# Moving two slabs of sure tokens ahead of the last row sums, with more filler behind them and a fixed hand-over to the experts

## The chip, the cores and the metric

The kernel runs on one core of a Trainium2 chip. The metric is the device time of one execution in microseconds (us); several executions are timed in rounds next to executions of the kernel before on the same chip. A ratio is the mean time of one kernel's fast runs over that of the other's fast runs of the same rounds, so it is not quite the ratio of the medians that are quoted. All runs told here were classed fast, that is, within 1.5% of the fastest of the same kernel. The kernel before shows two clusters among its fast runs, about 262.8 and about 263.9 us.

The engines: PE is TensorE's matmul, DVE VectorE, ACT ScalarE, POOL GpSimd (which issues most of the transfers here), SP the sync engine. PSUM is the memory, in banks, into which matmuls write and from which ACT and DVE copy. Moments are us from the start of the profiled execution.

## The reference

Attention with a linear bias and a sparse mask (8 global keys and a local window of 96) gives 3072 tokens of 512 numbers; a balanced router then hands each token to one of eight experts, 384 tokens each, in the order of all logits; each expert is a two-layer network.

```python
scores = q @ k.T / sqrt(D) - slopes * dist          # only global or local keys kept
x = softmax(scores) @ v                             # 3072 tokens x 512
order = argsort(-(x @ w_gate).flatten())
for idx in order:                                   # each token once, at most 384 a expert
    tok, e = idx // E, idx % E
    if assigned[tok] < 0 and counts[e] < cap: assigned[tok] = e; counts[e] += 1
for e in range(8):
    out[assigned == e] = relu(x[assigned == e] @ w1[e]) @ w2[e]
```

## The kernel before

The tokens of the first batches are known before the last batch's attention is done. So for five experts a first slab of 128 "sure" tokens is picked early (names with E at the end): small matmuls find their ids, an indirect DMA gathers each slab, PE transposes it, and its two layers (up, down) are used as filler for PE while the router's rounds wait for DVE. Cuts are marked "# ...".

```python
def e8_pe(q4):                       # one of three groups of six small matmuls: the ids
    # ...
def e8_ids():                        # two DVE ops, then one gather for each of four slabs
    # ...
    for e in range(ER): early_rows(e)

# the end of attention, in fixed order
            pr = sums(13)
            sums_out(13, pr)
            mask(15, 2)
            for g in range(3):
                attend(14, g)
                e8_pe(g)
            # ...
            e8_ids()
            pr = sums(14)
            # ...
            av(15)
            # ...
            pr = sums(15)            # 48 sum matmuls, then 8 for the gates
            sums_out(15, pr)

# filler: a list of (price in us, action); work(us) takes items until the price is spent
def rows(e):    # 4 transposes of slab e, ACT copies them to SBUF, price 0.25; two PSUM buffers
def up_one(...) # one matmul of the first layer, price 0.078; ACT applies relu after 16
def down_one(...)  # one matmul of the second layer, price 0.22; ACT evicts after 8
def work(us):
    while us > 0.0:
        cost, go = items.pop(0); go(); us -= cost

# the router: work(0.7), four rounds, the dispatch
def fast_round(k, X, Dg):            # PE -> DVE -> PE -> DVE ..., filler in between
    # ... work(0.34), work(1.0 or 1.1), comparisons tg on DVE, then
            work(0.7)
dispatch()                           # ids of all tokens, work(3.2) inside
for e in range(ER): gather(e, range(1, TSLAB), False)
# ...
while items: work(0.1)               # what is left of the filler

# the experts, outside the fixed order: the scheduler places the transposes
load_x(0)                            # slabs 1 and 2 of expert 0: transpose, DVE copy
```

The third expert's weights, two loads of 1 MB, are issued by POOL about 118.9 and 119.7 us, before the gathers of the sure slabs.

The softmax here doesn't subtract the row's maximum and nothing guards it: scores larger than these inputs give would overflow.

## Time and profile before

| | |
|---|---|
| median | 262.9 us (262.85 to 263.75) |
| span of the profiled run, clock | 261.1 us, 0.99 |
| PE busy | 242.8 us, 93% |
| last row sums end, router's first matmul (pkn) | 142.77, 144.54 |
| rounds one; two to four | 5.27; 15.88 us |
| last sure down matmul has been issued; experts start | 180.49; 182.62 |

### The profile page before, as it was taken

To read this page: it belongs to the slowest core of one execution; us is meant where nothing else is said; L and a number is where in the kernel's file an instruction comes from. 1 tells how busy PE (TensorE), PEld (TensorE's weight loads), DVE (VectorE), ACT (ScalarE), POOL (GpSimd) and SP (SyncE) were. 2 spreads that over 40 slices of the span, in tenths; PEclk is the share of its full clock that TensorE was granted. 3 is DMA by queue.
4 is the path that set the end of the run, shared out by engine and by line. 5 is a ranking of instruction groups with operands and counts; after the bars stand their busy time and mean duration, and the time that the engine had idled before them with its cause. 6 is when DMAs were issued, how large, how long until landed. Compare 5 with 4: busy or idle time off the path is not lost.

```text
span 261.1 us, 7832 instructions
## 1 busy us (share of the span) xinstructions
PE 242.8 (93%) x3319; PEld 179.9 (69%) x3331; DVE 163.0 (62%) x347; ACT 144.1 (55%) x245; POOL 87.9 (34%) x147
## 2 busy tenths in 40 slices
PE   8799979999999999999999899998999999999960
PEld 2567867888788888887787677664777765555520
DVE  3987998897978989689873877771223223223120
ACT  5998959679596895963442422233444432441600
POOL 5050000030270592014008400147865684541240
PEclk9999999999999999999999999999999999999996
DMA  6993597659698498949996999923799999991221
GB/s 261 335 318 76 165 251 209 189 103 270 177 248 239 93 292 188 208 93 148 210 211 143 155 188 215 241 95 102 132 242 268 276 240 229 201 281 41 89 84 46
DMA packets 52570, 49.29 MB, mean 189 GB/s; under 512 B 29745, under 2 KB 44081, under 8 KB 52529
## 3 DMA queue, kind: packets, MB, share of 16 engines
q0 software_dynamic: 15680, 26.22, 48.9%
q1 hardware_dynamic: 36848, 22.50, 31.2%
q8 instruction: 28, 0.46, 0.7%
q14 instruction: 14, 0.11, 0.1%
HBM read 56.05 MB, written 9.44 MB: 251 GB/s over the span
## 4 chain that ended last, share of the span: by engine, by line
PE 48%; DVE 20%; issue 10%; ACT 8%; DMA 6%; POOL 4%; POOLq 0%; SPq 0%; DVEq 0%
PE po L443 9%; PE ps L390 7%; PE ph L1375 5%; DVE RT L330 5%; DVE P L423 5%; PE po L1384 5%; PE pr L474 5%; DMA out_dram<-ot,idi 4%; POOL out_dram L945 4%; PE pk L519 3%; PE poE L988 3%; DMA RT<-in_q_dram 2%; ACT qT L355 2%; PE phE L972 2%; ACT P L408 2%
## 5 line engine op out<-in xcount | busy, mean ns | idle before, releaser
L408 ACT ACTIVATE P<-ps 128x860 f32<-128x860 f32 (+1 forms) x46 | 39.2, 891 | 23.1 <-PE ps L390 22.4
L1378 ACT ACTIVATE hT<-ph 128x256 bf16<-128x256 f32 (+1 forms) x64 | 27.1, 423 | 39.3 <-PE ph L1375 37.3
L390 PE MATMUL ps<-qT,kA 32*128 32x215 f32 (+2 forms) x864 | 43.3, 333 | 1.6 <-ACT qT L355 1.6
L443 PE MATMUL po<-P,v 128*64 128x215 f32 (+6 forms) x576 | 41.5, 293 | 0.2 <-DVE P L423 0.2
L390 PEld LDWEIGHTS ps<-qT,kA 32*128 32x128 f32 x864 | 36.8, 185 | 6.2 <-issue 2.8
L443 PEld LDWEIGHTS po<-P,v 128*64 128x64 f32 x576 | 34.0, 136 | 8.7 <-issue 3.8
L423 DVE TENSOR_TENSOR P<-P,Wm 128x860 f32<-128x860 f32 (+1 forms) x32 | 32.9, 1043 | 6.6 <-ACT P L408 3.9
L330 DVE STREAM_TRANSPOSE RT<-RT 128x768 f32<-128x768 f32 x28 | 26.2, 959 | 3.5 <-DMA RT<-in_k_dram 3.4
L474 PE MATMUL pr<-P,onesx 128*32 128x168 f32 (+11 forms) x768 | 27.6, 259 | 0.0
L1391 DVE COPY ot<-po 128x512 f32<-128x512 f32 x18 | 12.4, 691 | 24.1 <-PE po L1384 24.1
L945 POOL DMA_INDIRECT out_dram<-ot,idi x19 | 18.7, 983 | 26.0 <-DVE ot L1391 20.0
L1355 DVE COPY xT<-pxe 128x512 bf16<-128x512 bf16 x19 | 7.4, 421 | 31.6 <-PE pxe L1354 31.1
L474 PEld LDWEIGHTS pr<-P,onesx 128*32 128x32 f32 x768 | 24.7, 109 | 2.3 <-issue 0.3
L1384 PEld LDWEIGHTS <-hT 128*128 128x128 bf16 x152 | 14.4, 98 | 15.5
L340 ACT COPY kA<-RT 128x720 f32<-128x720 f32 (+2 forms) x18 | 24.3, 1352 | 0.2
L1375 PE MATMUL ph<-xT,w 128*128 128x384 bf16 (+1 forms) x160 | 23.4, 305 | 0.0
L1384 PE MATMUL po<-w,hT 128*128 128x512 bf16 x99 | 22.8, 379 | 0.2
L937 POOL DMA_INDIRECT xe<-x_tok,idi x19 | 18.3, 962 | 10.8 <-issue 4.3
L448 ACT COPY oT<-po 128x384 f32<-128x384 f32 x32 | 14.7, 486 | 11.4 <-PE po L443 11.4
L1375 PEld LDWEIGHTS <-w 128*128 128x128 bf16 x160 | 15.6, 98 | 7.7
L416 DVE TENSOR_TENSOR P<-P,Wm 128x860 f32<-128x860 f32 x16 | 16.4, 1058 | 6.7 <-ACT P L408 6.7
L519 PE MATMUL pk<-ident,oT 128*128 128x128 f32 x96 | 16.7, 288 | 2.4 <-DVE LT L490 2.2
(241 smaller groups left out, 328.1 us busy)
## 6 DMA issues: line engine op xcount, KB each, us to landing
w<-in_moe_w_dram POOLq DMA_DIRECT2D x10, 1024.0 KB, 12.2
v<-in_v_dram SPq DMA_DIRECT2D x32, 180.0 KB
RT<-in_k_dram SPq DMA_DIRECT2D x7, 768.0 KB
RT<-in_q_dram SPq DMA_DIRECT2D x7, 768.0 KB
w_early<-in_moe_w_dram POOLq DMA_DIRECT2D x8, 512.0 KB, 7.9
x_tok<-x SPq DMA_DIRECT2D x32, 96.0 KB
RT<-in_moe_w_dram POOLq DMA_DIRECT2D x2, 1024.0 KB, 18.3
w_early<-in_k_dram SPq DMA_DIRECT2D x1, 768.0 KB
```

The source lines that it names most:

```text
L330: nc.vector.transpose(out=t, in_=src[:, :, 32 * g : 32 * g + 32])
L340: nc.scalar.copy(out=kA[:, i0:i1, 8:128].rearrange("p i (c j) -> p i c j", j=NJ), in_=t[:, i0 * NC5 : i1 * NC5, :].rearrange("p (i c) j -> ...
L390: nc.tensor.matmul(heads[a][:, o : o + w], lhsT=kA[r, gd, i, :], rhs=qTt[r, gd, KT * i : KT * i + w], start=(gd == 0), stop=(gd == 1), ski ...
L408: nc.scalar.activation(P[:, :, 0 : GW[g]], ps[w_][:, :, 0 : GW[g]], AF.Exp, scale=0.125)
L423: tt(out=P[:, :, 0 : GW[g]], in0=P[:, :, 0 : GW[g]], in1=Wm[:, h0 : h0 + 2, lo : lo + GW[g]], op=ALU.mult)
L443: nc.tensor.matmul(po[n][bk][64 * t : 64 * t + 64, a - QB * bk : z - QB * bk], lhsT=v7[:, t, i, :], rhs=P[:, t, o + a - q0 : o + z - q0], ...
L474: nc.tensor.matmul(o_, lhsT=l_, rhs=r_, start=first[gq], stop=True, skip_group_check=True)
L519: nc.tensor.transpose(pk[:, bb, :], oTs[n][:, 3 * hf + bb].rearrange("c g r -> c (g r)"), ident)
L945: s = nc.gpsimd.indirect_dma_start(out=out[:, :], out_offset=bass.IndirectOffsetOnAxis(ap=ids, axis=0), in_=ot, in_offset=None)
L1375: nc.tensor.matmul(ph[:, 0 : 128 * ns], lhsT=w1_of(e)[:, kc, 128 * fc : 128 * fc + 128], rhs=xT_e[:, kc, 0:ns, :].rearrange("p t n -> p (t ...
L1378: nc.scalar.activation(hT[:, fc, 0 : 128 * ns], ph[:, 0 : 128 * ns], AF.Relu)
L1384: nc.tensor.matmul(po, lhsT=hT[:, fc, 128 * j : 128 * j + 128], rhs=w2_of(e)[:, fc, :], start=(fc == 0), stop=(fc == NFC - 1))
```

## The change

Its intent: have the ids of the sure slabs two us sooner, so that two slabs can be transposed ahead of the last row sums; with those out of the way, have up matmuls ready as filler in front of round one and in its waits; and transpose the first expert's own slabs in fixed order while the last filler runs. The whole diff, but for lines that only move a declaration:

```diff
@@ the end of attention
             pr = sums(13)
+            e8_pe(0)
+            e8_pe(1)
             sums_out(13, pr)
+            attend(14, 0)
+            e8_pe(2)
+            e8_ids()
             mask(15, 2)
-            for g in range(3):
-                attend(14, g)
-                e8_pe(g)
+            attend(14, 1)
+            attend(14, 2)
             oT_out(14, 0)
             oT_out(14, 1)
-            e8_ids()
             pr = sums(14)
             sums_out(14, pr)
             e7_flags()
             av(15)
+            px = ps_s.tile([128, 2, NKC, 128], BF16, tag="ps0", name="px")
+            for e in range(2):
+                for kc in range(NKC):
+                    nc.tensor.transpose(px[:, e, kc, :], xe_early[e][:, 128 * kc : 128 * kc + 128], ident_bf)
             oT_out(15, 0)
             oT_out(15, 1)
+            for e in range(2):
+                nc.scalar.copy(out=xT_early[e], in_=px[:, e])
             pr = sums(15)
@@ the order of the filler
-        for e in range(ER):
-            rows(e)
-        for f, e in ((up, 0), (up, 1), (down, 0), ...
+        for f, e in ((rows, 2), (up, 0), (rows, 3), (up, 1), (down, 0), ...
@@ a round
             for k0 in range(0, k, 4):
+                if k > 4:
+                    work(0.3)
                 nc.vector.tensor_tensor(   # tg
@@
-            work(0.7)
+            work(0.9)
@@ ahead of round one
-            work(0.7)
+            work(1.5)
@@ the tail
+            while len(items) > 4:
+                work(0.1)
+            rows_of_first(1, "pk")
             while items:
                 work(0.1)
+            rows_of_first(2, "pr2")      # 4 transposes into a free bank, DVE copy
@@ the experts
-            load_x(0)
             if not first:
                 gather(0, slabs(0))
+                load_x(0)
```

More of the change, by code (lines that the diff above doesn't have):

```diff
@@ L930 @@
     xes = {}
+    xT_of = {}
     scatters = []
@@ L999, in down @@
                 down_one(e, fc)
-        for e in range(ER):
-            rows(e)
-        for f, e in ((up, 0), (up, 1), (down, 0), (up, 2), (down, 1), (rows, 4), (up, 3), (down, 2), (up, 4), (down, 3),
-                     (down, 4)):
+        for f, e in ((rows, 2), (up, 0), (rows, 3), (up, 1), (down, 0), (up, 2), (down, 1), (rows, 4), (up, 3), (down, 2),
+                     (up, 4), (down, 3), (down, 4)):
             f(e)
@@ L1331, in routing, with rows_of_first @@
             nc.vector.tensor_single_scalar(out=fi, in_=fm, scalar=0.0, op=ALU.is_gt)
+            def rows_of_first(t, tag):
+                if t == 1:
+                    xT_of[0] = fp.tile([128, NKC, TSLAB, 128], BF16, tag="xT_e", name="xT_0")
+                xe = xes.pop(t)
+                pxe = ps_d.tile([128, NKC, 128], BF16, tag=tag, name=f"pxe{t}")
+                for kc in range(NKC):
+                    nc.tensor.transpose(pxe[:, kc, :], xe[:, 128 * kc : 128 * kc + 128], ident_bf)
+                nc.vector.tensor_copy(out=xT_of[0][:, :, t - 1, :], in_=pxe)
+            while len(items) > 4:
+                work(0.1)
+            rows_of_first(1, "pk")
             while items:
                 work(0.1)
+            rows_of_first(2, "pr2")
             while deferred:
@@ L1342, in experts @@
             ps_o = fctx.enter_context(tc.tile_pool(name="ps_o", bufs=3, space=bass.MemoryType.PSUM))
-            xT_of = {}
             def slabs(e):
@@ L1359, in experts @@
                 gather(0, slabs(0))
-            load_x(0)
-            if not first:
+                load_x(0)
                 gather(1, slabs(1))
```

## The prediction

> **What bounds the kernel now.** I read the page first, then the chain of work that ended last in order of time, then the time windows around the router, then the waits of TensorE. The page says TensorE is the engine:
>
> ```profile
> PE 242.8 (93%) x3319; PEld 179.9 (69%) x3331; DVE 163.0 (62%) x347; ACT 144.1 (55%) x245; POOL 87.9 (34%) x147
> ...
> PE   8799979999999999999999899998999999999960
> ```
>
> PE is near full in every slice, so a change pays only where it takes idle time off PE; moving its work about pays nothing by itself. From 182.62 us, where the experts' first matmul starts, to 250 us the windows show PE busy 66.95 of 67.38 us; after that only the last eviction, scatter and landing follow. So the end is the start of the experts plus a constant, and the question is how much earlier that start (182.6) comes. The windows in front of it (columns: window, its length, then busy time and count per engine; the first pair is PE):
>
> ```profile
> 138.32:140.78 2.46, 2.46 (x40) 2.15 (x37) 1.76 (x6) 0.48 (x1) 1.95 (x2) 1.00 0.72 168
> 140.78:142.77 1.99, 1.99 (x60) 1.61 (x57) 0.00 (x0) 0.48 (x1) 1.42 (x2) 1.00 0.27 80
> 142.77:144.54 1.77, 1.00 (x15) 0.73 (x13) 1.39 (x6) 1.28 (x3) 1.77 (x3) 1.00 0.43 134
> 144.54:149.81 5.27, 4.61 (x52) 3.81 (x52) 4.39 (x16) 1.82 (x5) 2.17 (x4) 1.00 1.01 154
> 149.81:155.05 5.24, 5.07 (x55) 4.12 (x56) 4.21 (x17) 1.43 (x5) 0.00 (x0) 1.00 1.16 184
> 155.05:160.35 5.30, 5.22 (x48) 3.88 (x49) 4.31 (x17) 1.56 (x4) 0.00 (x0) 1.00 1.17 213
> 160.35:165.69 5.34, 5.17 (x54) 3.99 (x53) 4.15 (x17) 1.51 (x4) 1.14 (x2) 1.00 1.17 214
> ...
> 180.66:182.62 1.96, 0.93 (x12) 0.75 (x12) 0.76 (x2) 0.58 (x1) 1.50 (x2) 1.00 0.46 134
> ```
>
> Attention (to 142.77) leaves PE no gap. The idle time is 0.77 before the router's first round, 0.66 in that round, 0.17, 0.08 and 0.17 in the other three, about 0.3 spread over 165.7 to 180.7, and 1.03 at the hand-over to the experts: 3.2 us in all. That is the most this change can earn. Who PE waited for, between 126 and 190 us:
>
> ```profile
> PE pxe L1354 <- ACT otE L992: 0.7, 1, 0.7
> PE px L959 <- ACT RT L960: 0.5, 1, 0.5
> PE prk L1117 <- DVE tg L1111: 0.4, 2, 0.2
> PE pxe L1354 <- DVE xT L1355: 0.4, 1, 0.4
> PE pkn L1075 <- DVE Lb L505: 0.3, 1, 0.3
> PE X L1060 <- DVE Dg L1138: 0.2, 1, 0.2
> ```
>
> And the hand-over in the chain (start, length, what): the last sure-token matmul, its eviction, the first transposes that wait for that eviction, their copy, then the experts.
>
> ```profile
> 179.19 1.47 PE poE L988 x6
> 180.69 0.59 ACT otE L992
> 181.33 0.40 PE pxe L1354 x4
> 181.82 0.43 DVE xT L1355
> 182.29 0.38 PE pxe L1354 x4
> 182.68 3.60 PE ph L1375 x32
> ```
>
> **What the Trainium skill says.** "TensorE: Matmul & The Clock Gate", section "Wait — 56ns, not 53.3ns?", gives a warm start-to-start of 55.6 ns for 128 columns and 215.7 for 512. The trace agrees: 32 up matmuls (phE) take 1.79 us in the chain, 56 ns each, and nine down matmuls (poE) take 1.94 us, 216 ns each. The same page, "Part 4: PE-mode transpose": the result lands in PSUM and needs a copy. Here four transposes take 0.22 us of PE and the copy 0.42 us on DVE or 0.58 on ACT; that copy is the price of the hand-over. "Perfetto Trace Analysis", section "Tensor Engine Instruction", says PE's ends are modelled: a matmul of 56 ns is recorded as 219 ns here, so busy time hides part of each gap, and I count from start to start below. "DMA: Bandwidth & Descriptors", section "Queues, rings and completion order": each DMA engine consumes a ring in order. The gathers of the sure tokens stand behind the third expert's weights, issued by the same engine at 119.0 and 119.7; the second of these took 20.6 us to land (about 140.3), and DMA share is above 1.1 until 139 us. So ids two us sooner need not mean rows two us sooner.
>
> **The change part by part.**
>
> 1. Ids. Now idiE is done at 136.81 and the first gather issues at 137.10. Moved up, the three id groups (0.38 us of PE each in the chain) run at sums(13)'s end, 132.45: two groups 0.76, attend(14,0) 0.88, last group 0.38, so about 134.5; two DVE ops (0.17 each) give ids at about 134.95, 1.9 sooner. DVE's mask(15,2) moves from 133.91 to about 135.0 and is wanted near 139.9. PE does the same work in another order. Gain by itself: 0.
>
> 2. Two slabs transposed before sums(15). Eight transposes, 0.44 us, now lie ahead of the last row sums, so the router's DVE chain (LT to Lb, then pkn at 144.54) moves to about 144.98. They leave the queue of filler behind it. This is a cost of 0.44 on the chain, bought back by part 3.
>
> 3. The gap before round one. From sums(15)'s end to pkn there are 1.66 us. Before, three slabs (0.66 us of PE, with a 0.5 us stall for the third slab's PSUM buffer) fill it. After: one slab (0.22), then 1.25 of nominal budget at 0.078 is 17 up matmuls, 0.95 us. Work done there 1.17, of which the chain paid 0.44 as shift: net 1.17 + 0.44 - 0.66 - 0.44 = 0.51 us gained.
>
> 4. Round one. It takes eight candidates, so DVE's two tg comparisons (1.29 us) and the selection bound it. Filler before: one slab plus 10 ups, then 9 ups: 1.28 us. After: 13 ups 0.73; 0.3 is two ups and a slab 0.33; 0.3 is four ups 0.22; 0.9 is twelve ups 0.67: 1.95. The extra 0.67 lies almost wholly in the 0.66 that PE waits. The fourth slab now sits between two uses of the same two PSUM buffers, so the second expert's first up waits some 0.25 us for the ACT relu; it falls inside DVE's comparison. Gain about 0.6.
>
> 5. Rounds two to four. Each has 0.2 more budget, and the order is further on (more downs at 216 ns). Estimated filler 1.93, 1.96, 1.99 us against 1.62, 1.98, 1.78 now; idle there is 0.42 in sum. Gain about 0.25; the rest lengthens rounds by 0.1 to 0.2, which costs nothing as it shortens the tail. Ids of the main dispatch come about 0.9 later than now (173.68 to about 174.6).
>
> 6. Hand-over. The last down matmul has been issued by 180.49; the experts start at 182.62: 2.13 us, in it 12 transposes (0.66), so 1.47 lost. After: slab one is transposed four downs before the end, slab two right behind the last down into a bank freed long before. From slab two's start, copy begins 0.49 later (as 181.33 to 181.82 now), takes 0.42, and a matmul starts 0.04 on: 0.97, in it 0.22 of work. Lost: 0.75, or 0.53 if the next expert's slab slips into the gap. Gain 0.7 to 0.95, say 0.8.
>
> Sum: 0.51 + 0.6 + 0.25 + 0.8 = 2.2 us. I take off 0.2 for a late slab (below) and small stalls: 262.9 - 2.0 = 260.9 us. Experts would start near 180.6.
>
> **The rivals.**
>
> Rival A, the rows are late. The two slabs are wanted at 140.8 and 141.0. If the gathers must drain behind the weights (until 139 to 140.3), slab two lands at an estimated 140.3 to 141.3, and PE stalls up to 0.5 us before sums(15), straight on the chain. For it: the DMA share. Against it: now the fifth gather lands 2.7 us after issue, the queue is then empty, and each gather moves only 0.13 MB. It would leave 261.3.
>
> Rival B, the gather of the first expert's own rows becomes the wait. Their ids come 0.9 later and their use 1 us sooner. Gathers land 2.7 to 2.8 us after issue, one issues each 1.27 us: slab one lands near 177.6, wanted near 178.7; slab two lands near 178.9, wanted near 179.8. Room of about 1 us; if it fails, up to 0.5 us is given back: 261.4.
>
> Rival C, nothing moves: the added filler delays the DVE chain as much as it shortens the tail. True of rounds three and four, where PE is full, but not of the gaps in parts 3, 4 and 6, where PE stands still. It would leave 262.9.
>
> Rival D, the experts are bound by weights and swallow the gain. Against it: the last weights issue at 222.6, land in about 12 us, and are wanted at 247; PE has no gap there now.
>
> **Range and chances.** The ceiling of 3.2 us gives 259.7; losing the hand-over or round one plus a late slab gives about 262. The runs before spread 0.9 us. Eight in ten: 260.0 to 262.2. Two per cent is 5.3 us, more than all the idle time there is, so faster by 2% gets 0.02; slower by 2% would need a new wait of 5 us, 0.02; within 2% 0.96.
>
> **What would show it.** Right: idiE near 135; pkn near 145.0; round one still about 5.3 us long with some 0.6 more PE work; no PE wait for tg or Dg; first expert matmul near 180.6 and about 1.0 us after slab two's transposes start; PE's busy time unchanged. Wrong: a PE wait for a DMA before the transposes near 141 (rival A) or 179 (rival B); rounds longer by what the tail loses (rival C); idle PE among the experts (rival D).

## The result, and the profile after

The changed kernel takes 261.33 us (261.25 to 261.93), the kernel before in the same rounds 262.88; the ratio is 0.9939 with a 95% interval of 0.9913 to 0.9964. That is 1.55 us less, within 2%, where 2.0 had been predicted. The experts start at 180.85 and not 182.62, 1.77 sooner; 0.2 of it is given back because one slab of the second expert is no longer transposed in front of them.

First the windows of the changed kernel (window, length, PE busy and count, then the other engines): attention's end, the last row sums, the gap ahead of round one, round one, two to four, and the hand-over.

```profile
140.50:142.03 1.53, 0.76 (x11) 0.46 (x9) 0.00 (x0) 0.48 (x1) 1.21 (x3) 1.00 0.37 107
142.03:144.02 1.99, 1.99 (x59) 1.60 (x57) 0.00 (x0) 1.07 (x2) 1.99 (x3) 1.00 0.59 86
144.02:145.80 1.78, 1.34 (x25) 1.20 (x22) 1.40 (x6) 1.04 (x2) 1.22 (x3) 1.00 0.99 153
145.80:151.01 5.21, 5.04 (x63) 4.54 (x63) 4.39 (x16) 1.74 (x5) 0.00 (x0) 1.00 1.11 191
151.01:156.53 5.52, 5.49 (x53) 4.11 (x50) 4.49 (x17) 1.67 (x4) 0.00 (x0) 1.00 1.21 208
156.53:161.72 5.19, 5.07 (x58) 4.20 (x56) 3.98 (x17) 1.56 (x4) 1.14 (x2) 1.00 1.11 201
161.72:167.29 5.57, 5.54 (x48) 4.05 (x47) 4.20 (x17) 1.35 (x4) 0.00 (x0) 1.00 1.21 227
...
180.16:180.85 0.69, 0.17 (x4) 0.00 (x1) 0.42 (x1) 0.57 (x1) 0.39 (x2) 1.00 0.18 71
```

The first line is new: in a stretch where PE had no gap before, it now stands still for half of 1.53 us. The other lines show the reverse: round one has 0.17 us of idle PE and not 0.66. Who PE waited for between 126 and 190 us, in the changed kernel (who, for whom: us, times, longest):

```profile
PE px L891 <- DMA RT<-x_tok,idiE: 0.8, 1, 0.8
PE ph L1395 <- DVE xT L1349: 0.5, 1, 0.5
PE pkn L1083 <- DVE Lb L505: 0.4, 1, 0.4
PE pc L1157 <- DVE M L1316: 0.3, 1, 0.3
PE phE L982 <- ACT hTE L985: 0.2, 1, 0.2
```

The waits for the comparisons tg, for Dg, for the third slab's buffer and for the eviction otE, which the view of the kernel before lists, are gone. In their place stands a wait for a DMA, the gather of a sure slab, and the hand-over waits for the slab's copy alone. That hand-over in the chain of the changed kernel (start, length, what):

```profile
179.25 0.86 PE poE L998 x4
180.11 0.24 PE pxe L1348 x4
...
180.37 0.44 DVE xT L1349
...
180.85 3.67 PE ph L1395 x32
```

Slab two's transposes start at 179.95 by the timeline and the experts 0.90 us later; before, 2.13 us lay between the last down matmul and the experts.

Counted from start to start (an up matmul 0.056 us, a down 0.216, a slab 0.22, times the counts in the two timelines), the 1.77 us divide like this (rounded):

| stage | before, us | after, us | filler in it, before and after | gained |
|---|---|---|---|---|
| up to the first matmul of round one | ends 144.54 | ends 145.80 | 0.66, 1.61 (with the two slabs moved forward) | -0.31 |
| round one | 5.27 | 5.21 | 1.28, 1.95 | 0.73 |
| rounds two to four | 15.88 | 16.28 | 5.38, 6.70 | 0.92 |
| from there to the experts | 16.93 | 13.56 | 2.95 less left to do | 0.42 |

The first row is the part that names the change, and it loses. The last row holds the hand-over, which by itself lost 1.47 us of PE before and 0.68 now, so about 0.8 gained, and 0.2 more from the slab that now comes after the experts' start; some 0.6 of new small waits take most of that back (0.28 for the dispatch mask M and some 0.25 between the two pf matmuls, at 175.51 and 175.85, are those that the timeline shows).

### The profile page after: what moved, and what is told of

The parts are those of the page before. It is cut to its first block, busy times and chain, and to the rows that moved or that the text cites.

```text
span 259.5 us, 7844 instructions
## 1 busy us (share of the span) xinstructions
PE 241.5 (93%) x3331; PEld 180.0 (69%) x3331; DVE 163.0 (63%) x347; ACT 144.0 (55%) x245; POOL 88.3 (34%) x147
## 4 chain that ended last, share of the span: by engine, by line
PE 43%; DVE 20%; DMA 13%; issue 9%; ACT 8%; POOL 3%; SPq 1%; POOLq 0%; DVEq 0%
PE ph L1395 7%; PE po L443 6%; PE ps L390 6%; PE po L1404 5%; DVE RT L330 5%; DVE P L423 5%; DMA x_tok<-x 4%; DMA out_dram<-ot,idi 4%; POOL out_dram L955 3%; PE poE L998 3%; PE pr L474 3%; PE pk L519 3%; PE phE L982 2%; DMA RT<-x_tok,idiE 2%; DMA RT<-in_q_dram 2%
## 5 line engine op out<-in xcount | busy, mean ns | idle before, releaser
L474 PE MATMUL pr<-P,onesx 128*32 128x192 f32 (+11 forms) x768 | 27.6, 259 | 0.0
L1404 PE MATMUL po<-w,hT 128*128 128x512 bf16 x104 | 23.8, 379 | 0.0
L1376 DVE COPY xT<-pxe 128x512 bf16<-128x512 bf16 x17 | 6.6, 421 | 26.0 <-PE pxe L1375 25.6
```

Of the source, the lines that this page charges most:

```text
L474: nc.tensor.matmul(o_, lhsT=l_, rhs=r_, start=first[gq], stop=True, skip_group_check=True)
L1404: nc.tensor.matmul(po, lhsT=hT[:, fc, 128 * j : 128 * j + 128], rhs=w2_of(e)[:, fc, :], start=(fc == 0), stop=(fc == NFC - 1))
```

## The experiments

Theory W: the slabs land when the third expert's weights, which stand ahead of them in the same queue, are through; ids two us sooner do not move that, so PE waits. Theory I: the slabs land a fixed time after their ids, and the early ids are what makes the early slabs possible. Beside these stands the question which part gained: named part, filler or hand-over.

### e1_ids_late: the ids in their old order

```diff
-            e8_pe(0); e8_pe(1); sums_out(13, pr); attend(14, 0); e8_pe(2); e8_ids()
-            mask(15, 2); attend(14, 1); attend(14, 2)
+            sums_out(13, pr); mask(15, 2)
+            for g in range(3): attend(14, g); e8_pe(g)
             oT_out(14, 0); oT_out(14, 1)
+            e8_ids()
```

> The changed kernel with the ids back in their old order (groups between the attend groups, ids after both oT copies, so about 136.8 us and first gather about 137.1), everything else changed. Theory W (the weights of the third expert, ahead in the same queue, set when the rows land, whatever the ids do): the two slabs still land near 141.3, PE waits 0.7 to 1.0 us in front of them, time 261.2 to 261.6 us, level with the changed kernel. Theory I (rows land a fixed time after their ids): they land 1.9 us later, PE waits about 2.6 us, time about 263.2 us.

Measured: 261.54 us (261.18 to 263.88), ratio 0.9956 (0.9922 to 0.9990), level with the changed kernel. The profiled execution was one of the late kind: everything from 56 us on is 0.8 to 0.9 later, the weights too. In the POOL timeline of this run, the weights' issue and the first gather, and PE's start of the slabs:

```profile
119.83 1.66 POOL L840 DMA_DIRECT2D RT<-in_moe_w_dram  x2
137.92 1.09 POOL L659 DMA_INDIRECT RT<-x_tok,idiE  x1 [16.44 <-DVE idiE L654]
```

```profile
142.29 0.75 PE L888 MATMUL px<-ident_bf,RT 128*128 128x128 bf16 x8 [0.63 <-DMA RT<-x_tok,idiE]
```

And in the changed kernel:

```profile
118.95 1.66 POOL L840 DMA_DIRECT2D RT<-in_moe_w_dram  x2
135.09 1.63 POOL L659 DMA_INDIRECT RT<-x_tok,idiE  x1 [14.48 <-DVE idiE L654]
```

```profile
141.33 0.77 PE L891 MATMUL px<-ident_bf,RT 128*128 128x128 bf16 x8 [0.78 <-DMA RT<-x_tok,idiE]
```

From the weights' issue (119.83 here, 118.9 there) to PE's start of the slabs: 22.5 and 22.4 us, the same. From the first gather's issue: 4.4 and 6.2 us, so the gather issued 1.9 us sooner, relative to the weights, arrived no sooner. Theory I, with 263.2 us, is out. (In e4b, below, the two distances are 22.1 and 5.9 us.)

### e2_w2_behind: the second weight load behind the gathers

```diff
-            for dst, src in zip(w_2, (w1 of expert 2, w2 of expert 2)):
-                nc.gpsimd.dma_start(dst, src)
+            nc.gpsimd.dma_start(w_2[0], w1 of expert 2)
 ...
     early_rows(ER)
+    nc.gpsimd.dma_start(w_2[1], w2 of expert 2)
     for _ in range(4): late_weights(False)
```

> The changed kernel with the second weight load of the third expert (its w2, 1 MB) issued after the five gathers and not in front of them. Theory W: the queue is empty of weights when the gathers come, each lands 2.6 to 2.8 us after issue, the 0.78 us wait of PE in front of the two slabs is gone, experts start near 180.1, time 260.4 to 260.7 us. Theory I or any theory in which the gather itself is slow: wait and time stay at 0.8 and 261.3 us. If the late w2 is late for its down matmuls, a PE wait for it appears near 170 us; I do not expect it.

Measured: 263.98 us (262.96 to 264.58), ratio 1.0029 (1.0005 to 1.0053): slower than the kernel before, so the time I expected was wrong. The first half came as expected: PE starts the two slabs at 140.44 without a wait and pkn at 144.75, a us sooner than in the changed kernel. So the second weight load did set when they landed. But a wait comes back later; from the waits of PE in this run:

```profile
PE pxe L1347 <- DMA xe<-x_tok,idi: 2.7, 1, 2.7
PE ph L1394 <- DVE xT L1348: 0.5, 1, 0.5
```

PE waits 2.7 us for the first expert's own rows. Their gather is not slow, it lands 2.9 us after its issue; it is issued late. POOL in this run, and below it in the changed kernel:

```profile
177.76 0.99 POOL L946 DMA_INDIRECT xe<-x_tok,idi  x1 [4.56 <-DMA x_tok<-x]
...
175.56 0.99 POOL L947 DMA_INDIRECT xe<-x_tok,idi  x1 [1.31 <-DVE vt L1324]
```

Here the ids are ready at 174.24, and POOL waits 3.5 us longer for the last stores of x_tok, the attention's rows, from which this gather reads. SP issues these stores, in another queue. They are recorded with 8.9 us to landing, and with 3.1 in the changed kernel. From 172 to 174 us the busy share of the DMA engines is 1.20 here and 0.00 in the changed kernel. The likely reason is that the 1 MB moved behind the sure gathers keeps the engines busy that long; no run shows that by itself. The stop has a second cost: the granted clock is 0.50 from 182 to 184 us, and the 32 up matmuls of the first expert take 4.40 us and not 3.67. So this wait is the one that rival B of the prediction names, reached by another way: the rows to be gathered were late, not the ids. And because stores in another queue are late too, e2 does not tell whether the sure gathers had waited for their turn in the queue or for busy engines; no run here does.

### e3_px_mid: the two slabs between the sums and the gates

```diff
+        def sums(n, between=None):
 ...
+            if between is not None: between()      # the 8 transposes
             for o_, l_, r_ in gates:
 ...
-            (the transposes ahead of sums(15), the ACT copies ahead of it)
+            pr = sums(15, px_rows)
+            (the ACT copies after it)
```

> The changed kernel with the eight transposes of the two slabs moved from the front of the last row sums to between its 46 sums and its 8 gate matmuls, about 1.6 us later on PE. Theory W (rows land at 141.3, PE wanted them at 140.5): PE reaches them at about 142.1, the wait of 0.78 us is gone, pkn starts near 145.0 and not 145.8, time 260.4 to 260.7 us. A theory in which PE waited for something that moves with the transposes (their PSUM bank): the wait follows them and the time stays 261.3 us.

Measured: 260.58 us (260.33 to 260.61), ratio 0.9905 (0.9885 to 0.9925): 2.3 us faster than before and 0.75 faster than the changed kernel (measured in other rounds; e1, level with it, took 261.54 in the same ones), and the fastest kernel of this study on the chips where the kernel before takes 262.9. PE reaches the slabs at 142.07 with no wait, pkn starts at 145.08. A new wait appears, for the copies of the two slabs, which hold the bank that the third slab's transposes go to:

```profile
PE px L974 <- ACT RT L901: 0.8, 1, 0.8
PE ph L1400 <- DVE xT L1354: 0.5, 1, 0.5
```

It takes the place of the 0.4 us that PE waited for DVE's Lb in the changed kernel, which is gone. The wait for the gather was thus worth about what the waits view says, 0.8 us, and moving the consumer past the landing gets it back.

### e12_mid_ids_late: the same with the late ids

The edits of the first and the third experiment together.

> The slabs between sums and gates, with the ids in their old, late order. Theory W (the weights in front set the landing, near 141.3): the slabs are there at 142.1 all the same, no wait, 260.4 to 260.8 us, level with the run that has the early ids. Theory I (ids set it): the second slab lands near 141.1 to 141.3 on its own 2.7 us after its issue at 138.4, so here both theories allow no wait for the two slabs; the third slab lands near 142.4, before it is wanted. A time above 261.2 us would say that the early ids buy something after all.

Measured: 260.81 us (260.54 to 261.87), ratio 0.9912 (0.9887 to 0.9937). No wait for the two slabs or for the third one's gather (PE starts the two at 142.47). Both theories had expected that, so it is e1 that decides between them, and early ids buy nothing here by an earlier landing. They may buy 0.2 us in another way: in the early order of the id groups PE takes 0.25 us less for the same matmuls (see the last section), and e3's median is 0.23 below this one. In the changed kernel the wait for the landing swallows that. As the two runs were on two chips, it is not settled.

### e5_hand_only: the hand-over alone, on the kernel before

```diff
+            while len(items) > 4: work(0.1)
+            rows_of_first(1, "pk")
             while items: work(0.1)
+            rows_of_first(2, "pr2")
 ...
-            load_x(0)          # in the experts
```

> The kernel before with the hand-over alone changed: the first expert's slab one transposed four downs before the end, slab two behind the last down, in fixed order. My sum gave this part 0.7 to 0.95 us: time 261.9 to 262.2 us, experts about 0.9 us after slab two's transposes start. Rival: a part of it is only moved, since the next expert's slab no longer goes in front of the experts' first matmul (0.22 us): experts start 1.0 to 1.2 sooner but the time falls only 0.8 to 1.0, 261.9 to 262.1. Rival B (the gathers are late): a PE wait for a DMA near 179 us and less than 0.5 us gained.

Measured: 262.00 us (261.85 to 262.16), ratio 0.9960 (0.9942 to 0.9978), so 0.89 us. The experts start at 181.54, 0.90 after slab two's transposes at 180.64; the waits for the eviction otE and the second wait for xT are gone and one of 0.5 for the copy is left. No PE wait for a DMA, so rival B plays no part.

### e4_px_only, e6_fill_only, e9_fill_hand and e10_px30_two on another chip

These four ran together on a chip where the kernel before takes 274.73 us (273.55 to 275.70). Their edits: e4 takes the change without the budgets and the hand-over; e6 takes the budgets alone on the kernel before; e9 takes budgets and hand-over without ids and early slabs; e10 is e3 with the transposes after 16 of the 24 sums and

```diff
-            while items: work(0.1)
+            while len(items) > 2: work(0.1)
             rows_of_first(2, "pr2")
+            while items: work(0.1)
```

> The part of the change that names it, alone: ids early and two slabs transposed ahead of the last row sums, with the old filler budgets and the old hand-over. From the traces so far: PE waits 0.8 us for the first slab, pkn moves from 144.54 to about 145.8 (1.26 us later), and by then 1.0 us of filler is done and not 0.66; net loss about 0.9 us, time 263.6 to 263.9 us. If my prediction's own term were right (no wait, 0.44 of shift paid back by 0.44 less filler), 262.8 to 263.0 us.

> The kernel before with the larger filler budgets alone (1.5 and not 0.7 ahead of round one, 0.3 twice ahead of the two comparisons of round one, 0.9 and not 0.7 in every round); the slabs stay behind the row sums. My sum gave round one 0.6 and the later rounds 0.25; the gap ahead of round one now holds four slabs that wait for two PSUM buffers, so it gains little there: time 261.9 to 262.3 us, no PE wait for the comparisons. If filler only moves time from the tail into the rounds (the rival that nothing moves): 262.7 to 263.0 us.

> The whole change without the early ids and the early slabs: the larger budgets and the fixed hand-over on the kernel before. If the named part gains nothing, or loses what the filler behind it gains, this is level with the changed kernel: 260.9 to 261.5 us. If early ids and slabs carry the gain, it stays at 262.0 us or above.

> From the run with the slabs transposed between sums and gates (260.58): here they come after 16 of the 24 sums (PE at about 141.5, just behind the landing at 141.3), so that their copies are done before the third slab needs the PSUM bank (that wait of 0.75 us should go), and slab two of the first expert is transposed two downs before the end, so that its copy of 0.42 us runs beside two matmuls. If the copy is what PE waits for at the hand-over, 0.3 to 0.4 us less: 260.1 to 260.4 us; the gather of slab two (lands about 2.8 us after issue) then leaves PE a wait of 0.1 us or so. If the landing of the rows is 0.3 us later than the trace shows, PE waits for it in the middle of the sums and the gain is smaller.

Measured, against 274.73: e4 273.55 us, ratio 0.9960; e6 271.23, 0.9876; e9 270.40, 0.9854; e10 267.66, 0.9738. None of the times I had expected can be compared, for this chip has stops that the others do not show. They lie at the hand-over and in the first expert: PE stands still for 4.65 us in e4, for 3.58 in e9, for 1.0 in e6, and three times for 0.8 in e10, and the trace names neither an engine nor a transfer for them. In e9:

```profile
182.39 0.39 PE L1341 MATMUL pxe<-ident_bf,xe 128*128 128x128 bf16 x4
185.88 0.42 DVE L1342 COPY xT<-pxe 128x512 bf16<-128x512 bf16 x1 [2.42 <-remote]
186.36 3.77 PE L1388 MATMUL ph<-xT,w_early 128*128 128x256 bf16 x20 [3.58 <-issue]
```

PE's stop ends with DVE's copy of slab two, but that copy starts 3.1 us after its transposes have ended, and what it waited for, called remote, is not named further. The same kernel on the next chip starts the experts 0.9 us after those transposes. What makes this chip slower stays open, and the parts are not read from it.

### e9b_fill_hand: filler and hand-over without the named part

> The same kernel as in the run of this name without the b, whose chip ran every kernel, the one before too, about 12 us slower, with waits of PE among the experts that the other chip has not shown. On a chip where the kernel before takes about 262.9 us: if the named part of the change (early ids, early slabs) gains nothing, or loses what the filler behind it gains, this is level with the changed kernel, 260.9 to 261.5 us; if that part carries gain, 262.0 us or above.

Measured: 261.45 us (260.89 to 262.87), ratio 0.9942 (0.9912 to 0.9971), against 0.9939 for the whole change. So the change without early ids and early slabs is as fast as the change, within intervals of some 0.7 us each way. The traces are finer: from the issue of the third expert's weights to the start of the experts it takes 61.63 us and the changed kernel 61.90, so the named part gains nothing here and may cost 0.3.

### e4b_px_only: the named part alone

> The same kernel as in the run of this name without the b, again for a chip where the kernel before takes about 262.9 us. Theory W: PE waits 0.8 us for the first slab, pkn about 1.26 us later, 0.34 us more filler done by then, net loss about 0.9 us, time 263.6 to 263.9 us. My prediction's own term (0.44 of shift paid back, no wait): 262.8 to 263.0 us.

Measured: 263.97 us (263.85 to 264.83), ratio 1.0033 (1.0010 to 1.0056): 1.03 us slower than the kernel before, a tenth beyond theory W's range and well outside that of the prediction's own term. Its waits:

```profile
PE pkn L1083 <- DVE Lb L505: 1.0, 1, 1.0
...
PE px L891 <- DMA RT<-x_tok,idiE: 0.5, 1, 0.5
```

The slabs are late by 0.5 us at the first (141.05) and their eight transposes take 0.86 us from start to start where e3's take 0.55, which fits a second slab that came later still; and the gap ahead of pkn, without the larger budget, leaves PE idle for 1.0 us.

### e11_px30_two_fill: an attempt at a still faster version

As e10, with work(1.9) for work(1.5) ahead of round one and for work(1.6) ahead of the dispatch mask.

> The kernel with the slabs after 16 of the 24 sums and slab two of the first expert two downs before the end, plus larger budgets where the changed kernel's PE still waited (1.9 and not 1.5 ahead of round one, 1.9 and not 1.6 ahead of the dispatch mask). On a chip where the kernel before takes about 262.9 us: 0.3 to 0.4 from the copy beside the downs, 0.2 to 0.3 from the two fillers, against the 260.58 us of the run with the slabs between sums and gates: 259.8 to 260.2 us. If the gather of slab two binds (ids about 2.9 us before it is wanted), PE waits for a DMA near 178.5 and the time is 260.2 to 260.5.

Measured: 261.65 us (260.93 to 262.58), ratio 0.9936 (0.9908 to 0.9964): a miss, by the medians a us slower than e3 and 0.8 slower than e12 of the same rounds. Part of that is chance: the profiled execution is of the late kind, and from the weights' issue to the experts' start it takes 61.55 us where e3 takes 61.05, so the kernel loses about 0.5 and the early part of the execution the rest. Two waits explain where the expected gain went:

```profile
PE ph L1404 <- ACT otE L1009: 0.7, 1, 0.7
PE pxe L1355 <- DMA xe<-x_tok,idi: 0.6, 1, 0.6
```

Transposed two downs earlier, slab two's copy does lie beside matmuls. But the experts' first matmul then waits 0.7 us for the eviction of the last down (I take it for the PSUM bank, as that wait stood before the hand-over in the kernel before), which had been hidden behind the copy. And slab two is now wanted before its gather has landed, since more filler in the rounds leaves less of it after the ids: rival B after all. How much of the loss each of the three edits carries was not separated.

## Why the prediction was right or wrong

The time was predicted as 260.9 in a range of 260.0 to 262.2, and 261.33 was measured. The direction was right, and so was that it stays within 2%. That the sum came so near is partly luck: parts 2 and 3 together came out 0.8 below the forecast and part 5 0.7 above it.

- What bounds the kernel: right. PE stays full among the experts (67.55 us busy of 67.55 from 180.85 to 248.4 us), and the time follows the experts' start.
- Part 1, ids worth nothing by themselves: right in the changed kernel, by e1. That PE does the same work in another order is not quite so: the other order takes it 0.25 us less, which shows only where no wait follows (e12 against e3). The ids came at 134.8; that the rows need not come sooner for it, e1 shows.
- Part 2, "Eight transposes, 0.44 us, now lie ahead of the last row sums": this term was mis-sized. The chain moved by 1.26 us and not 0.44. 0.78 is the wait for the landing (rival A: the prediction held it possible at "up to 0.5 us" and took off 0.2 for it and for small stalls; its sign, a PE wait for a DMA near 141, came true), and the transposes took 0.70 from start to start in the changed kernel and 0.55 in e3.
- Part 3, the gap: the filler came out as counted, a slab and 17 ups, and the wait for the third slab's buffer went. The step "net ... 0.51 us gained" failed with part 2: the row of the stage table is -0.31. Neither experiment shows a gain: the named part alone loses 1.03 us, where without the larger budget PE idles ahead of pkn, and on top of filler and hand-over it is worth about nothing (0.9939 against 0.9942).
- Part 4, round one: predicted 0.6, and 0.73 by the stage table. The wait for the second expert's up was 0.17 us in the trace, not 0.25, and the waits for tg and Dg went.
- Part 5, rounds two to four: predicted 0.25, 0.92 by the stage table. This term was mis-sized the other way: filler in them rose by 1.32 us, not by 0.5, while the rounds grew by 0.40 together. The 0.42 of idle time that the windows showed was taken as the ceiling, but ends of matmuls are modelled and hide gaps; the prediction names that and then used the windows' figure all the same.
- Part 6, the hand-over: predicted 0.8, measured 0.89 alone (e5). Copy and start came as laid out, 0.90 after the transposes' start where 0.97 was counted.
- Rival B stayed off in the change itself; its wait came in e11, and in e2 by way of the stores of x_tok. Rival C, added filler that only moves time, is refuted by the rows of round one to four in the stage table and by e9b, which is faster than e5. Rival D did not occur on the chip of the prediction; the slow chip is open.

The share of the filler alone was not measured on a chip that runs the kernel before in 262.9 us; e9b less e5 leaves about 0.6 us for it by the medians, taken across two chips, and 1.0 us by the traces (from the weights' issue to the experts' start 61.63 and 62.60 us; the kernel before takes 63.62, e4b 64.51).

## What to carry to other kernels

Before you make a producer's command earlier, look at what already stands in the queue that will carry it: the landing may be set by the transfers in front, and then it is the consumer that has to move, here by 1.6 us, behind the landing. Taking the load out of the way instead can cost more later, as in e2, even by way of another queue. Test a change with several parts by its parts: the part that named this one did not pay, while the filler and the fixed hand-over carried the time. When you hide the last wait of a hand-over, look for the one hidden behind it, and for the gather that was only just in time.

## What the Trainium skill lacked or had wrong

- "DMA: Bandwidth & Descriptors", section "Queues, rings and completion order", says, where it speaks of the queues of SP and ACT, that each engine consumes a ring in order; it has no figure for a small gather behind a large load, both issued by POOL. Here the slab started 22.1 to 22.5 us after the weights' issue, whether its own gather had been issued 4.4, 5.9 or 6.2 us before; with no load ahead a gather lands in 2.6 to 2.8 us. The order in the ring fits that, but no run tells it apart from busy engines.
- "TensorE: Matmul & The Clock Gate", "Part 4: PE-mode transpose", has about 275 ns for a transpose in a kernel and says that the full clock does not engage for it. Here a transpose is recorded with 216 to 219 ns, four take 0.22 us from start to start in a row, and the granted clock in those windows is 1.00. They stand among other matmuls; transposes alone were not run.
- "Perfetto Trace Analysis" says that matmul ends are estimated; it does not say how much idle time that hides. In rounds two to four the windows showed 0.42 us of idle PE before and 0.18 after, yet 1.32 us more filler went in while the rounds grew by 0.40: about 0.7 us of room that no busy time showed.
- "TensorEngine Tiling (Array Packing)", "Key Properties", says that changing the tiling mode drains TensorE, but has no figure for it. Here the attention and id matmuls are recorded as 128*64 and 128*128. Three groups of six id matmuls, each between attention matmuls, made that stretch 3.89 us (132.45 to 136.34); with two of the groups in a row it is 3.63 us for the same instructions (132.41 to 136.04), with two changes of kind fewer. The runs with either order repeat these lengths (e1 3.88, e2 3.63); that the changes cause the difference is not shown.
- No page read prepares for two chips that differ so: the kernel before took 262.9 us on three chips and 274.7 on a fourth. Its cause is open.
